# Two small bias loads and the first projection weights, moved to the tail of SyncE's start-up queue in a token-mixing transformer kernel

## The chip, the cores and the metric

The kernel runs on one core of one Trainium2 chip. The metric is device time in microseconds (us) for one execution of the whole kernel; lower is better. Before the change it is 1309.34 us, the median of 3 runs (1308.7 to 1309.64).

## What is computed

Input `x` has S = 2048 tokens of D = 1024 values in bfloat16. Four blocks follow one another, attention and token MLP in turn, with the same weights in both rounds:

```
x = x + A(layernorm(x), wqkv, wo)
x = x + B(layernorm(x), w1, b1, w2, b2)
x = x + A(layernorm(x), wqkv, wo)
x = x + B(layernorm(x), w1, b1, w2, b2)

A: qkv = x @ wqkv; 32 heads of 32 values; each token attends to itself and
   7 earlier tokens, 2 apart (positions s, s-2, ..., s-14); softmax; then @ wo
B: h = layernorm(x); u = gelu(h transposed @ w1 + b1)   (mixes over tokens, F = 3584)
   y = u @ w2 + b2; transposed back
```

`b1` has 3584 values and `b2` has 2048, both bfloat16. They are used in B alone: `b1` in the gelu, `b2` in the last sum. The first block that needs them is the second of the four.

## The kernel before

The tokens are cut into 16 tiles of 128 (even tokens first, then odd ones, because attention steps by two). A round has these stages: the projection to v for all 16 tiles; attention in 16 units, in which the q and k projections (`qk_chunk`, L345) of the next unit are interleaved with the scores and values of the present one; the output projection (`out_proj`, L435); the first MLP matrix (`gemm1`, L462) and the second (`gemm2`, L506). TensorE does all the products; ScalarE (ACT) and VectorE (DVE) empty its PSUM buffers and do softmax, gelu and layernorm; SyncE (SP) issues nearly all DMAs.

The change is in the first round's start (`start_up`, L202 to L319). It carries each token tile k through these steps, whose short names are functions in the code:

- `x_load` (L208): SP loads tile k of x, 256 KB (tile 0 in two halves). `w_load` (L217): SP loads a quarter of the v weights, 512 KB, tile name `wv`.
- `S_` (L221, twice per tile) and `A_` (L226): DVE computes mean and variance (`bn`, `mv`).
- `R_` (L230, through L172 and L173): ACT computes one over the standard deviation (`rs`).
- `N_` (L234, through L186): DVE normalises the tile in place.
- For tiles 0 to 4, `tr` (L239) transposes on TensorE (PE), and `C_` (L245) copies the result to `hT` on ACT. For tiles 5 to 15, `T_` (L263) is a transposing DMA, issued by SP, straight into `hT`.
- `V_` (L251): PE, 8 products for each half n of v. `E_` (L259): ACT empties that PSUM buffer (two buffers, tile name `m`).

Before any of this PE runs 14 warm-up products on zeros (L268).

The order on each engine is written out by hand: lists `pe`, `act`, `dve` and `sp` (L285 to L304) are worked off by the loop at L310, and `chain_` (L198) ties every step to the step issued before it on the same engine. So an engine can't do a later step of its list while it waits for an earlier one. Two things matter in the lists: DVE has `S_` of tile k + 1 (first half) ahead of `N_` of tile k, and ACT has a long run of `E_` and `R_` in turn.

What isn't tied by `chain_` is placed by the Tile framework's scheduler, where it finds the engine free by its own estimate. Before the change that holds for two things called right after `start_up` (L532 to L534):

- `load_qk(0)` (L337): SP loads the q and the k weights of the first four attention units, 512 KB each, tile name `wqk`. `qk_chunk` reads them when attention begins.
- `load_biases` (L138): GpSimd (POOL) issues the loads of `b1` and `b2` into bfloat16 tiles (`b_bf` in the profile), and DVE casts them to float32 (`b_sb`; L142 and L143). Both tiles lay a vector out over 128 partitions, 28 values of b1 and 16 of b2 in each, from a source in which neighbours in a partition lie 256 bytes apart (pairs of b2 excepted):

```
nc.gpsimd.dma_start(out=b1_bf[:], in_=B_b1.rearrange("(t p) -> p t", p=P))
nc.gpsimd.dma_start(out=b2_bf[:], in_=B_b2.rearrange("(i m c) -> m i c", m=P, c=DIL))
nc.vector.tensor_copy(out=b1_sb[:], in_=b1_bf[:])
nc.vector.tensor_copy(out=b2_sb[:], in_=b2_bf[:])
```

Later `load_qk` calls (L554) load the next weights as attention goes on; they aren't tied either. Weights of all kinds share a pool of 9 buffers. The last item on DVE's list is `zero_fill` (L149), which clears borders of attention's buffers.

Of the kernel before, what the change touches and what calls it, by code (L numbers as in the profile page):

```python
# [14 lines left out]
P = 128  # L15
# [3 lines left out]
DIL = 2  # L19
# [6 lines left out]
def kernel(  # L26
# [15 lines left out]
    nc = tc.nc  # L42
    x_in = A_x[0]
    out2d = out[0]
    S, D = x_in.shape
    F = B_w1.shape[1]
    KD = D // P
    FT = F // P
    NT = S // P
# [55 lines left out]
    def wt_(name, shape):  # L105
        return wp.tile(shape, BF16, name=name, tag="w")
# [4 lines left out]
    def ln_exp_table():  # L111
        return tc.keep_in_program_order(nc.scalar.preload_act_table_set("natural_log_exp_and_others"))
# [20 lines left out]
    b1_bf = const.tile([P, FT], BF16, name="b1_bf")  # L133
    b2_bf = const.tile([P, NI, DIL], BF16, name="b2_bf")
    b1_sb = const.tile([P, FT], FP32, name="b1_sb")
    b2_sb = const.tile([P, NI, DIL], FP32, name="b2_sb")

    def load_biases():  # L138
        with nc.allow_non_contiguous_dma(reason="tiny bias loads"):
            nc.gpsimd.dma_start(out=b1_bf[:], in_=B_b1.rearrange("(t p) -> p t", p=P))  # L140
            nc.gpsimd.dma_start(out=b2_bf[:], in_=B_b2.rearrange("(i m c) -> m i c", m=P, c=DIL))
        nc.vector.tensor_copy(out=b1_sb[:], in_=b1_bf[:])  # L142
        nc.vector.tensor_copy(out=b2_sb[:], in_=b2_bf[:])  # L143

    hT = pers.tile([P, KD, S], BF16, name="hT")
    qT = [pers.tile([P, S + PAD], BF16, name=f"qT{n}") for n in range(2)]
# [15 lines left out]
    wq_v = A_wqkv.rearrange("(kt p) c -> p kt c", p=P)  # L162
# [4 lines left out]
    def rows(t, c, i):  # L167
        return t[(c * NI + i) * P:(c * NI + i + 1) * P, :]
# [29 lines left out]
    def chain_(eng, f, *args):  # L198
        with tc.issue_after(last[eng].ins) if eng in last else nullcontext():
            last[eng] = f(*args)  # L200

    def start_up(v, wv):  # L202
        np_ = 5
        warm = x2("warm", [P, 512])
        nc.vector.memset(warm[:], 0.0)
        xs, tps, pss_, mvs, sts, rss = {}, {}, {}, {}, {}, {}
# [88 lines left out]
        dve = [(S_, 0, 0), (S_, 0, 1), (A_, 0)]  # L295
        for k in range(NT):
# [4 lines left out]
            if nx:  # L301
                dve += [(S_, k + 1, 1), (A_, k + 1)]
        dve.append((zero_fill,))
        sp = [(T_, k) for k in range(np_, NT)]  # L304
        qs = {"PE": pe, "ACT": act, "DVE": dve, "SP": sp}
        need = {R_: lambda k: k in mvs, N_: lambda k, h: k in rss, tr: lambda k: (N_, k) in done, C_: lambda k: k in tps,
                V_: lambda k, n, kts: ((C_, k) in done or (T_, k) in done), E_: lambda k, n: (V_, k, n) in done,
                T_: lambda k: (N_, k) in done}
        done = set()
        while any(qs.values()):  # L310
            for eng, q in qs.items():
                while q and (q[0][0] not in need or need[q[0][0]](*q[0][1:])):
                    f, *args = q.pop(0)
                    chain_(eng, f, *args)
                    if f is V_:
                        if args[2][-1] == KD - 1:
                            done.add((f, args[0], args[1]))
                    elif args:
                        done.add((f, args[0]))  # L319

    def load_wv():
        return [[wt_("wv", [P, KD // 2, 512]) for _ in range(2)] for _ in range(NDC)]

    def fill_wv(wv, n):
        for hf in range(2):
            nc.sync.dma_start(out=wv[n][hf][:],
                              in_=wq_v[:, hf * (KD // 2):(hf + 1) * (KD // 2), 2 * D + n * 512:2 * D + (n + 1) * 512])

    def v_proj(v, c, i, wv, ns):
        for n in ns:  # L330
            ps = m_tile()
            for kt in range(KD):
                nc.tensor.matmul(ps[:], lhsT=hT[:, kt, cols(c, i)], rhs=wv[n][kt // 4][:, kt % 4, :],  # L333
                                 start=(kt == 0), stop=(kt == KD - 1))
            nc.scalar.copy(out=v[c][i][:, n * 512:(n + 1) * 512], in_=ps[:])

    def load_qk(g2):  # L337
        ts = []
        for part in range(2):
            t = wt_("wqk", [P, KD, 256])  # L340
            nc.sync.dma_start(out=t[:], in_=wq_v[:, :, part * D + g2 * 256:part * D + (g2 + 1) * 256])
            ts.append(t)
        return ts

    def qk_chunk(u, wts, part, n):  # L345
        g, c = divmod(u, DIL)
# [14 lines left out]
    def in_order(f, *args):  # L361
        with tc.issue_after(last_pe[0].ins) if last_pe[0] is not None else nullcontext():
            last_pe[0] = f(*args)
# [61 lines left out]
    def load_wo():  # L425
        tiles = []
        for n in range(NDC):
            tiles.append([])
            for hf in range(2):
                t = wt_("wo", [P, NG // 2, 512])  # L430
                nc.sync.dma_start(out=t[:], in_=wo_v[:, hf * (NG // 2):(hf + 1) * (NG // 2), n * 512:(n + 1) * 512])
                tiles[n].append(t)
        return tiles

    def out_proj(c, i, oT, wo, res, dst, h2):  # L435
        xr = x2("xr")
        nc.sync.dma_start(out=xr[:], in_=res(c, i))
        xn = x2("xn")
        for n in range(NDC):
            ps = m_tile()  # L440
            xs_ = slice(n * 512, (n + 1) * 512)
            for g in range(NG):
                mm = nc.tensor.matmul(ps[:], lhsT=oT[g][:, cols(c, i)], rhs=wo[n][g // 4][:, g % 4, :],  # L443
                                      start=(g == 0), stop=(g == NG - 1))
            nc.vector.tensor_tensor(out=xn[:, xs_], in0=ps[:], in1=xr[:, xs_], op=ALU.add)  # L445
        nc.sync.dma_start(out=rows(dst, c, i), in_=xn[:])
        h2[c][i] = vhp.tile([P, D], BF16, name="h2", tag="vh")
        mean, rs = stats(xn, 1.0 + EPS, eps2)
        norm_act(h2[c][i][:], xn[:], mean, rs)
        return mm  # L450
# [47 lines left out]
    def load_w2(i):  # L498
        tiles = []
        for n in range(NW2):  # L500
            t = wt_("w2", [P, HF, 256])
            nc.sync.dma_start(out=t[:], in_=w2_v[:, n * HF:(n + 1) * HF, i * 256:(i + 1) * 256])
            tiles.append(t)
        return tiles
# [20 lines left out]
    for li in range(2):  # L525
        first = li == 0
        v = [[None] * NI for _ in range(DIL)]
        for c, i in order:
            v[c][i] = vhp.tile([P, D], BF16, name="v", tag="vh")
        wv = load_wv()  # L530
        if first:
            start_up(v, wv)  # L532
            wts = load_qk(0)
            load_biases()  # L534
            res = lambda c, i: xin_v[c, i]
        else:
            fill_wv(wv, 0)
            fill_wv(wv, 1)
            wts = load_qk(0)
            for i in range(NI):  # L540
                for c in range(DIL):
                    v_proj(v, c, i, wv, (0, 1))
            res = lambda c, i: rows(xb, c, i)
        oT = [gop.tile([P, S], BF16, name="oT", tag="go") for _ in range(NG)]
        h2 = [[None] * NI for _ in range(DIL)]
        chunks = [(0, 0), (0, 1), (1, 0), (1, 1)]
        last_pe[0] = None
        for part, n in chunks:
            in_order(qk_chunk, 0, wts, part, n)
        wo = None  # L550
        for vis in range(2 * NU):
            u, b = divmod(vis, 2)
            if b == 0 and u + 1 < NU and (u + 1) % (2 * DIL) == 0:
                wts = load_qk((u + 1) // (2 * DIL))  # L554
            if vis == 2 * NU - 6:
                wo = load_wo()
            in_order(scores, u, b)
            for n in range(2):
                if n and vis:
                    in_order(values, *divmod(vis - 1, 2), v, oT)  # L560
                if u + 1 < NU:
                    in_order(qk_chunk, u + 1, wts, *chunks[2 * b + n])
                else:
                    in_order(out_proj, 0, 2 * b + n, oT, wo, res, xa[li], h2)
        in_order(values, NU - 1, 1, v, oT)
        for c, i in order[4:]:
            out_proj(c, i, oT, wo, res, xa[li], h2)
        g = [None] * NFB
        for fb in range(NFB):
            gemm1(fb, h2, g)  # L570
        if first:
            ln_exp_table()
        for i in range(NI):
            w2t = load_w2(i)
            for c in range(DIL):
                gemm2(c, i, w2t, g, xa[li], rows(xb, c, i) if first else out_v[c, i], first)
# [30 lines left out]
```

The softmax here doesn't subtract the row's maximum and nothing guards it: scores larger than these inputs give would overflow.

## Time and profile before

| What | Value |
|---|---|
| Median of 3 runs | 1309.34 us |
| The profiled execution, its time | 1308.38 us |
| Its span, first to last instruction | 1306.7 us |
| PE busy | 1294.7 us (99%) |
| DVE busy, ACT busy, POOL busy | 392.6, 385.1, 4.3 us |
| DMA, mean rate | 93 GB/s |
| First step of attention's q, k products (L350) | 73.59 us after the span's start |

The profile is of one execution. Its engines are PE (products), PEld (weight loads of PE), DVE, ACT, POOL and SP. A row of the timeline gives the start in us from the span's start, the duration, the engine, the line, the operation, the tile written and those read, the shape and the count; in square brackets stands how long the engine had been idle before it and what ended that wait. "SPq" or "POOL" with DMA_DIRECT2D is the issue of a DMA, not its transfer; a DMA's landing is when its completion is seen. PE's busy time counts pipelined products whose ends are modelled, so a busy PE isn't always a PE at its full rate.

### The profile page before, as it was taken

How to read it: one execution, taken by the hardware profiler on the slowest of the kernel's cores; microseconds unless marked ns; L12 is line 12 of the kernel's file. 1: busy time of each engine (PE TensorE's matmuls, PEld its weight loads, DVE VectorE, ACT ScalarE, POOL GpSimd, SP SyncE). 2: the span in 40 equal slices, each digit the busy share in tenths (PEclk: the TensorE clock that was granted, in tenths of full speed). 3: DMA queues.
4: the chain of work that ended last, by engine and by line, in shares of the span. 5: the costliest groups of instructions: out<-in, count | busy, mean ns of one | idle time of the engine just before them, and what ended most of it. 6: DMA issues, size and time to landing. Idle time of an engine off the chain costs nothing.

```text
span 1306.7 us, 21044 instructions
## 1 busy us (share of the span) xinstructions
PE 1294.7 (99%) x9398; PEld 583.0 (45%) x9398; DVE 392.6 (30%) x654; ACT 385.1 (29%) x628; POOL 4.3 (0%) x13
## 2 busy tenths in 40 slices
PE   7999999999999999999999999999999999999998
PEld 3444444444444444444444444444444444444443
DVE  5436667930000013223210566688000000111111
ACT  4446776531111110000023677664211111000000
POOL 1000000000000000000000000000000000000000
PEclk8999999999999999999999999999999999999999
DMA  9521112452322227456431100144522222334320
GB/s 250 113 66 34 34 34 83 145 170 65 93 68 71 76 67 180 113 136 172 121 89 37 53 27 19 35 130 151 147 65 81 81 59 72 110 105 133 117 91 33
DMA packets 191290, 121.69 MB, mean 93 GB/s; under 512 B 33376, under 2 KB 172896, under 8 KB 191200
## 3 DMA queue, kind: packets, MB, share of 16 engines
q1 hardware_dynamic: 191088, 120.35, 32.6%
q8 instruction: 73, 1.20, 0.4%
q0 software_dynamic: 112, 0.01, 0.1%
q14 instruction: 17, 0.14, 0.0%
HBM read 96.48 MB, written 16.78 MB: 87 GB/s over the span
## 4 chain that ended last, share of the span: by engine, by line
PE 95%; DVE 2%; ACT 1%; DMA 1%; issue 0%; POOL 0%; POOLq 0%
PE m L350 18%; PE s L513 15%; PE s L470 15%; PE m L513 7%; PE m L470 7%; PE acc L470 7%; PE acc L513 7%; PE m L443 7%; PE m L333 4%; PE m L255 3%; PE acc L404 1%; PE s L376 1%; PE acc L408 1%; DMA b_bf<-in_B_b_dram 1%; DVE xn L445 1%; DVE x L186 0%
## 5 line engine op out<-in xcount | busy, mean ns | idle before, releaser
L513 PEld LDWEIGHTS <-w 128*128 128x128 bf16 x1792 | 175.4, 98 | 211.4
L470 PEld LDWEIGHTS <-w 128*128 128x128 bf16 x1792 | 175.3, 98 | 211.5
L350 PE MATMUL m<-hT,wqk 128*128 128x512 bf16 x1024 | 241.8, 380 | 0.0
L470 PE MATMUL s<-h,w 128*128 128x512 bf16 x896 | 202.8, 379 | 0.0
L513 PE MATMUL s<-g,w 128*128 128x512 bf16 x896 | 199.9, 379 | 0.0
L516 DVE SCALAR_TENSOR_TENSOR xo<-s,b_sb,xs 128x512 bf16<-128x512 f32 x32 | 24.0, 751 | 540.7 <-PE s L513 534.4
L350 PEld LDWEIGHTS <-wqk 128*128 128x128 bf16 x1024 | 90.5, 98 | 108.7 <-issue 12.9
L385 DVE TENSOR_TENSOR Pm<-pc,band 64x1152 bf16<-64x1152 bf16 x128 | 96.3, 752 | 65.1 <-ACT pc L380 63.1
L443 PE MATMUL m<-wo,oT 128*128 128x512 bf16 x512 | 112.2, 379 | 0.1
L380 ACT ACTIVATE pc<-s,shift 128x576 bf16<-128x576 f32 x128 | 87.8, 737 | 59.9 <-PE s L376 59.9
L470 PE MATMUL acc<-h,w 128*128 128x512 bf16 x448 | 103.9, 379 | 0.0
L513 PE MATMUL acc<-g,w 128*128 128x512 bf16 x448 | 100.6, 379 | 0.0
L513 PE MATMUL m<-g,w 128*128 128x512 bf16 x448 | 99.3, 379 | 0.0
L470 PE MATMUL m<-h,w 128*128 128x512 bf16 x448 | 99.0, 379 | 0.0
L172 ACT ACTIVATE ln<-mv,eps 128x1 f32<-128x1 f32 x64 | 18.9, 295 | 240.4 <-DVE mv L180 222.2
L477 ACT ACTIVATE g<-s,b_sb 128x1024 bf16<-128x1024 f32 x28 | 31.2, 1114 | 166.9 <-PE s L470 166.9
L443 PEld LDWEIGHTS <-oT 128*128 128x128 bf16 x512 | 49.4, 98 | 59.6 <-issue 1.3
L255 PE MATMUL m<-wv,hT 128*128 128x512 bf16 x256 | 58.0, 383 | 1.2 <-ACT hT L248 0.7
L422 DVE TENSOR_TENSOR oT<-acc,rd 128x512 bf16<-128x512 f32 x64 | 44.0, 687 | 39.6 <-ACT rd L420 39.6
L333 PE MATMUL m<-wv,hT 128*128 128x512 bf16 x256 | 55.4, 379 | 0.0
L356 DVE CAST qT<-m 128x512 bf16<-128x512 f32 x32 | 21.8, 682 | 83.1 <-PE m L350 83.1
L445 DVE TENSOR_TENSOR xn<-m,xr 128x512 bf16<-128x512 f32 x64 | 44.0, 688 | 8.0 <-PE m L443 6.6
(61 smaller groups left out, 631.7 us busy)
## 6 DMA issues: line engine op xcount, KB each, us to landing
w<-in_B_w_dram SPq DMA_DIRECT2D x56, 512.0 KB, 3.8
w<-in_B_w_dram SPq DMA_DIRECT2D x64, 448.0 KB, 4.5
wqk<-in_A_wqkv_dram SPq DMA_DIRECT2D x16, 512.0 KB, 5.6
xa<-xn SPq DMA_DIRECT2D x32, 256.0 KB, 2.0
xs<-xa SPq DMA_DIRECT2D x32, 256.0 KB, 3.2
wv<-in_A_wqkv_dram SPq DMA_DIRECT2D x8, 512.0 KB, 5.3
wo<-in_A_wo_dram SPq DMA_DIRECT2D x8, 512.0 KB, 4.8
xr<-in_A_x_dram SPq DMA_DIRECT2D x16, 256.0 KB, 3.0
```

The source lines that it names most:

```text
L255: r = nc.tensor.matmul(pss_[k, n][:], lhsT=hT[:, kt, cols(*order[k])], rhs=wv[n][kt // 4][:, kt % 4, :], start=(kt == 0), stop=(kt == KD - 1))
L333: nc.tensor.matmul(ps[:], lhsT=hT[:, kt, cols(c, i)], rhs=wv[n][kt // 4][:, kt % 4, :], start=(kt == 0), stop=(kt == KD - 1))
L350: mm = nc.tensor.matmul(ps[:], lhsT=wts[part][:, kt, (g % 2) * P:(g % 2 + 1) * P], rhs=hT[:, kt, lo:lo + 512], start=(kt == 0), stop=(kt = ...
L380: nc.scalar.activation(out=pc[:, 2 * n:2 * n + 2].rearrange("p h t k -> p h (t k)"), in_=ss[n][:, :, 0:HB * HW], func=ACT.Exp, scale=scale ...
L385: nc.vector.tensor_tensor(out=pm[rp, :, b * HB:(b + 1) * HB, r * HK:r * HK + HW], in0=pc[rp], in1=mk, op=ALU.mult)
L422: nc.vector.tensor_tensor(out=oT[g][:, lo:lo + hb * P], in0=acc[:, 0, :], in1=rd[:], op=ALU.mult)
L443: mm = nc.tensor.matmul(ps[:], lhsT=oT[g][:, cols(c, i)], rhs=wo[n][g // 4][:, g % 4, :], start=(g == 0), stop=(g == NG - 1))
L445: nc.vector.tensor_tensor(out=xn[:, xs_], in0=ps[:], in1=xr[:, xs_], op=ALU.add)
L470: nc.tensor.matmul(pairs[fl][0][dc], lhsT=wt[c][:, i, fl * P:(fl + 1) * P], rhs=h2[c][i][:, dc * 512:(dc + 1) * 512], start=(k == 0), stop ...
L477: nc.scalar.activation(out=g[fb][:, fl, :].rearrange("p (n d) -> p n d", n=2), in_=t[:], func=ACT.Gelu_apprx_tanh, bias=b1_sb[:, ft:ft + 1])
L513: nc.tensor.matmul(aps[dc], lhsT=w2t[ft // HF][:, ft % HF, c::DIL], rhs=g[ft // GF][:, ft % GF, dc * 512:(dc + 1) * 512], start=(ft == 0), ...
L516: nc.vector.scalar_tensor_tensor(out=xo[:, dc * 512:(dc + 1) * 512], in0=aps[dc], scalar=b2_sb[:, i, c:c + 1], in1=xs[:, dc * 512:(dc + 1) ...
```

## The change

The two bias loads go from POOL's queue to SP's, and out of the scheduler's hands: they become the last item of SP's hand-written list, behind the transposing DMAs of all tiles. The two casts become a step of their own, the last of DVE's list, behind `zero_fill`; the loop's table of conditions holds it back until the loads have been issued in program order. `load_qk(0)` is tied to SP's chain as well, behind the bias loads. `load_qk` fills a list that it is given and returns its last DMA, as `chain_` wants it; its two later calls do what they did. The loop's `done` set now also takes steps without arguments.

```diff
     def load_biases():
         with nc.allow_non_contiguous_dma(reason="tiny bias loads"):
-            nc.gpsimd.dma_start(out=b1_bf[:], in_=B_b1.rearrange("(t p) -> p t", p=P))
-            nc.gpsimd.dma_start(out=b2_bf[:], in_=B_b2.rearrange("(i m c) -> m i c", m=P, c=DIL))
+            nc.sync.dma_start(out=b1_bf[:], in_=B_b1.rearrange("(t p) -> p t", p=P))
+            return nc.sync.dma_start(out=b2_bf[:], in_=B_b2.rearrange("(i m c) -> m i c", m=P, c=DIL))
+
+    def cast_biases():
         nc.vector.tensor_copy(out=b1_sb[:], in_=b1_bf[:])
-        nc.vector.tensor_copy(out=b2_sb[:], in_=b2_bf[:])
+        return nc.vector.tensor_copy(out=b2_sb[:], in_=b2_bf[:])
...
         dve.append((zero_fill,))
-        sp = [(T_, k) for k in range(np_, NT)]
+        dve.append((cast_biases,))
+        sp = [(T_, k) for k in range(np_, NT)] + [(load_biases,)]
...
-        need = {R_: lambda k: k in mvs, ...
+        need = {cast_biases: lambda: (load_biases,) in done, R_: lambda k: k in mvs, ...
...
-                    elif args:
-                        done.add((f, args[0]))
+                    else:
+                        done.add((f, *args[:1]))
...
-    def load_qk(g2):
-        ts = []
+    def load_qk(g2, ts):
         for part in range(2):
-            t = wt_("wqk", [P, KD, 256])
-            nc.sync.dma_start(out=t[:], in_=wq_v[:, :, part * D + g2 * 256:part * D + (g2 + 1) * 256])
-            ts.append(t)
-        return ts
+            ts[part] = wt_("wqk", [P, KD, 256])
+            r = nc.sync.dma_start(out=ts[part][:], in_=wq_v[:, :, part * D + g2 * 256:part * D + (g2 + 1) * 256])
+        return r
...
             start_up(v, wv)
-            wts = load_qk(0)
-            load_biases()
+            wts = [None, None]
+            chain_("SP", load_qk, 0, wts)
```

More of the change, by code (lines that the diff above doesn't have):

```diff
@@ L303, in start_up @@
         dve.append((zero_fill,))
-        sp = [(T_, k) for k in range(np_, NT)]
+        dve.append((cast_biases,))
+        sp = [(T_, k) for k in range(np_, NT)] + [(load_biases,)]
         qs = {"PE": pe, "ACT": act, "DVE": dve, "SP": sp}
-        need = {R_: lambda k: k in mvs, N_: lambda k, h: k in rss, tr: lambda k: (N_, k) in done, C_: lambda k: k in tps,
+        need = {cast_biases: lambda: (load_biases,) in done, R_: lambda k: k in mvs, N_: lambda k, h: k in rss, tr: lambda k: (N_, k) in done, C_: lambda k: k in tps,
                 V_: lambda k, n, kts: ((C_, k) in done or (T_, k) in done), E_: lambda k, n: (V_, k, n) in done,
@@ L538 @@
             fill_wv(wv, 1)
-            wts = load_qk(0)
+            wts = [None, None]
+            load_qk(0, wts)
             for i in range(NI):
@@ L553 @@
             if b == 0 and u + 1 < NU and (u + 1) % (2 * DIL) == 0:
-                wts = load_qk((u + 1) // (2 * DIL))
+                wts = [None, None]
+                load_qk((u + 1) // (2 * DIL), wts)
             if vis == 2 * NU - 6:
```

## The prediction, on record before the result

> **What bounds the kernel now.** I read the page first, then the chain of waits for the first 80 us, then DVE's timeline at the start, then a table of windows, then SP's queue. The page says that PE is the engine to ask about:
>
> ```profile
> PE 1294.7 (99%) x9398; PEld 583.0 (45%) x9398; DVE 392.6 (30%) x654; ACT 385.1 (29%) x628; POOL 4.3 (0%) x13
> ```
>
> The change touches only the start, so what counts is whether the start is late. The chain of waits (start, duration, what) begins with a bias load, which is odd for data first read at 287.2 us (the gelu of L477):
>
> ```profile
> 1.37 8.74 DMA b_bf<-in_B_b_dram
> 10.46 0.30 ACT ln L172
> 11.03 0.43 DVE x L186
> 11.50 1.05 PE s L242 x8
> ...
> 45.97 27.79 PE m L255 x128
> ```
>
> DVE's timeline shows how. Statistics of tile 0 are done at 4.33; their aggregation (L228), which alone lets ACT and then the normalisation go on, starts at 10.22, because the cast of b1 stands ahead of it and waits 5.81 us for its load:
>
> ```profile
> 3.04 1.29 DVE L224 BATCH_NORM_STATS2 bn<-x 128x6 f32<-128x512 bf16 x2 [1.71 <-DMA x<-in_A_x_dram]
> 10.13 0.18 DVE L142 CAST b_sb<-b_bf 128x28 f32<-128x28 bf16 x1 [5.81 <-DMA b_bf<-in_B_b_dram]
> 10.22 0.20 DVE L228 BATCH_NORM_AGGREGATE mv<-bn 128x2 f32<-128x12 f32 x1
> ```
>
> The windows (stretch, length, busy time of PE, PEld, DVE, ACT, POOL, then granted clock, DMA share, GB/s) show the price: warm-up to 6.65, then 4.85 us in which PE does nothing while DMA crawls at 167 GB/s, then the v projection to 73.75:
>
> ```profile
> 1.40:6.65 5.25, 5.25 (x14) 1.77 (x14) 1.29 (x2) 0.69 (x1) 3.72 (x7) 1.00 0.92 210
> 6.65:11.50 4.85, 0.00 (x1) 0.01 (x1) 1.32 (x5) 0.50 (x2) 0.00 (x0) 0.74 1.16 167
> 11.50:18.58 7.08, 5.97 (x36) 3.29 (x37) 4.63 (x11) 3.41 (x9) 0.00 (x0) 0.69 1.07 370
> 18.58:73.75 55.17, 54.69 (x264) 24.77 (x262) 27.50 (x57) 25.41 (x62) 0.00 (x0) 1.00 0.60 138
> ```
>
> From 27 to 46 us the chain alternates between DVE (L186, L224, L228) and ACT with a period of 1.99 us per tile (22.31, ..., 41.49, 43.49); from 45.97 PE runs 128 products back to back. Both parts hang on tile 0's aggregation, so a shift there goes through to attention, and from there PE is full to the end.
>
> [...] So b1 is 3584 descriptors of 2 bytes and b2 1024 of 4 (pairs lie together); over 16 engines 224 + 64 = 288 each. [...] the software queue has 80 data packets, of 128 and 64 bytes for b1 and 256 for b2. [...] bias packets run from 5.64 to 10.04 us, and the second quarter of `wv` landed 4.33 us after the first (7.18, 11.51), though 512 KB take 1.36 us at the rate of the later x tiles (256 KB every 0.68 us). So the biases cost the stream 4.33 - 1.36 = 2.97 us, 10.3 ns per descriptor. [...] products are 0.43 us apart until 5.6, again from 13.2 to 15.1, and 0.216 from 16.0 on.
>
> **The change part by part.**
>
> *The cast leaves the head of DVE's queue.* Recomputing the start with the trace's own durations: aggregation of tile 0 at 4.41 instead of 10.22; ACT's two steps end at 5.2. DVE's list has the first statistics of tile 1 ahead of the normalisation, and tile 1 lands at 5.17: statistics 5.2 (was 10.34), normalisation 5.89 (was 11.03). The first transpose could start 0.47 later, at 6.36, but PE ends its warm-up at 6.65: it starts there, 4.85 us earlier than at 11.50. The idle window is gone.
>
> *The bias transfers leave the early stream.* Everything from the second `wv` quarter on comes about 3.0 to 3.3 us earlier: that quarter at about 8.3, x tile 2 (was 12.18) at about 9.0, the last `wv` quarter (was 15.87) near 12.5. These landings move less than 4.85, so one may become the new wait. First copy of tile 0: 7.3 to 8.4; first v products at 7.95, with `wv` there since 7.18 at the latest. Normalisation of tile 1 needs ACT's rs at 8.84, but in DVE's list it stands behind tile 2's first statistics: 9.0 + 0.66 = 9.68, against 14.10. **Next late is x tile 2**, and the gain is 4.42 here. Then PE's clock gives some back: its first transposes follow the warm-up directly, and if it is still at full clock at 10.3, tile 1's transposes take 0.62 instead of 1.05 and the gain is 4.42 + 0.43, about 4.85; if the clock has dropped, 4.4 or a little more. Tile 2's normalisation (was 17.52) follows tile 1's copy, so it carries that gain. Tile 4 is wanted at 13.7 and lands near 13.1. From there the 1.99 us rhythm and the 128 products are the same. I take 4.8.
>
> *The load of wqk moves* from 19.27 and 19.96 to behind the last transposing DMA. That one was issued at 46.69 and took 1.29: SP is free at 47.98 - 4.8 = 43.2. Nothing was queued behind the old place (SP was idle until 26.14), so leaving it saves nothing. It is wanted by L350, at 73.59 - 4.8 = 68.8. It takes 5.6 us from issue to landing (median of 16). So the biases ahead of it may take 68.8 - 43.2 - 5.6 = 20.0 us, which is 69 ns for each of 288 descriptors. Their price in SP's queue isn't in the trace. Below: 10.3 ns, as now, 3.0 us. Nearest row: two `wqk` loads issued together land 1.66 us apart, 64 descriptors of 512 bytes per engine, 26 ns each: 7.5 us. Above: [...] doubling 26 gives an estimate of 52 ns, 15.0 us. I take 7.5; at all three the cost is nothing, as it lies under the v products. A gain below nothing is excluded, since these loads are only added there.
>
> *SP's issue* of 3584 and 1024 descriptors: 1024 took 0.37 (wqk) to 1.29 us (transpose), so by scale 1.7 to 5.8 us for both, within the same cover. Behind them on SP stands only wqk until PE frees weight buffers (next issue at 71.20).
>
> *The casts* (0.18 + 0.16 us) wait on DVE behind the zero fill, until about 43 + 7.5 + 3 = 54. Behind them is the first q copy (L356, at 77.25, before which DVE idles 26.64 us). No cost; without that cover a late bias would hold that copy.
>
> *POOL* loses 1.68 + 0.92 us of issues ahead of the identity and band masks (3.18 to 5.44). PE wants the identity at 6.65; no gain.
>
> **Sum**, on the profiled execution: 1308.38 - 4.8 = 1303.6 (span 1301.9). That execution is 0.96 under the median of the runs, so median 1309.34 - 4.8 = **1304.5**.
>
> **Rivals.**
>
> *Transfers come no earlier.* If the dip in the stream isn't the biases' doing, x tile 2 still lands at 12.18, tile 1 is normalised at 12.86 instead of 14.10, and the gain is about 1.3: 1308.0. [...] Against: it ran at over 300 GB/s between 4.5 and 6 us, and the dip's limits are those of the bias packets.
>
> *The biases hold wqk too long* (ends slower). SP sends single elements at a price above 69 ns; L350 then waits at the start of attention. From 86 ns on ((20.0 + 4.8) / 288) the gain is gone. At 100 ns the biases take 28.8 us, wqk is 8.8 late, and the sum is +4.0: 1313.3. For it: the price isn't in the trace[...]. Against: it needs nearly three times the price of a 512-byte packet.
>
> *The change doesn't do what it says*: the scheduler puts another load, one that waits for PE to free a buffer, ahead of wqk on SP, or another wait takes the cast's place on DVE. The first is excluded by the chain only for the tied steps. It would cost about what it gains: 1309.
>
> **How the numbers follow.** About 0.2%, 2.6 us, is what a measurement can tell from no change here. Main forecast 0.82 (faster); transfers no earlier 0.06 (same); not what it says 0.04 (same); biases too long 0.08 (slower, a small part same, neglected). Ends: if x tile 2 comes at 8.3 the rs of tile 1 decides and 14.10 becomes 8.84, gain 5.3, with the clock's 0.43 some 5.7: 1303.6, less 0.4 for the scatter of runs (1308.7 to 1309.64): 1303.2. If PE drops to half clock for one window of 3.4 us on the way, half of that is lost: gain 3.1, 1306.2, plus 0.4: 1306.6. The range is 1303.2 to 1306.6.
>
> **What would show it.** Right: in the after profile tile 0's aggregation follows its statistics with no gap; the first transpose is at about 6.65; no dip between 6 and 10 us; `wv`'s second quarter lands near 8.3; tile 1 is normalised at 9.7 behind tile 2's landing; L350 starts at 68.8; bias loads follow the last transpose near 43. Wrong: a wait of L350 for wqk at the start of attention, any DVE wait for b_bf that something else queues behind, or a first normalisation still late.

## The result

| | Before | After |
|---|---|---|
| Median | 1309.15 us (4 runs, 1308.7 to 1309.64) | 1303.55 us (4 runs, 1303.29 to 1303.78) |
| Profiled execution, span | 1308.38, 1306.7 | 1303.29, 1301.6 |
| Attention's first products | 73.59 (L350) | 68.70 (L351) |

The ratio is 0.9957 (95% interval 0.994 to 0.9974). The median moved by 5.6 us, the profiled execution by 5.1, the start of attention in it by 4.89; the forecast was 4.8. In the changed file most lines are one to three numbers further down: L172, L186, L224, L228, L341 and L350 are now L174, L188, L226, L230, L343 and L351.

DVE's timeline of the changed kernel at the start:

```profile
3.00 1.29 DVE L226 BATCH_NORM_STATS2 bn<-x 128x6 f32<-128x512 bf16 x2 [1.67 <-DMA x<-in_A_x_dram]
4.32 0.21 DVE L230 BATCH_NORM_AGGREGATE mv<-bn 128x2 f32<-128x12 f32 x1
5.11 0.69 DVE L226 BATCH_NORM_STATS2 bn<-x 128x6 f32<-128x512 bf16 x1 [0.58 <-DMA x<-in_A_x_dram]
...
9.24 0.69 DVE L226 BATCH_NORM_STATS2 bn<-x 128x6 f32<-128x512 bf16 x1 [1.96 <-DMA x<-in_A_x_dram]
9.85 0.53 DVE L188 TENSOR_SCALAR x<-x,mv,rs 128x1024 bf16<-128x1024 bf16 x1
```

The aggregation follows its statistics with no cast between. But DVE waits again, at 9.24, for x tile 2: the new wait that was forecast. It holds tile 1's normalisation (9.85) although its rs has been there since 8.43. The chain of waits agrees; its first long piece is no longer a bias load, but the load of x tile 2, issued at 3.21 (start, duration, what):

```profile
3.21 6.00 DMA x<-in_A_x_dram
9.28 0.57 issue
9.85 0.54 DVE x L188
...
67.41 1.46 PE m L257 x6
68.87 6.91 PE m L351 x32
```

The windows (columns as in the prediction) show what became of the dead stretch:

```profile
1.40:6.65 5.25, 5.25 (x21) 2.11 (x22) 3.04 (x7) 1.18 (x3) 0.99 (x5) 1.00 0.80 258
6.65:11.50 4.85, 2.34 (x19) 1.13 (x18) 2.82 (x7) 1.87 (x5) 0.00 (x0) 1.00 1.02 322
11.50:18.58 7.08, 6.58 (x42) 3.22 (x42) 5.32 (x11) 4.46 (x13) 0.00 (x0) 1.00 1.06 383
```

From 6.65 to 11.50 the DMA engines move 322 GB/s where it was 167, PE works for 2.34 us where it did nothing, and its clock stays at 1.00 (it was 0.74, then 0.69). A profile's record of the clock begins with the first rise (at 5.61 before, at 5.00 here), so the 1.00 of the first row says nothing of the time ahead of it, in which products come 0.43 us apart, as against 0.216 later.

SP's queue at the tail, with the biases between the last transpose and wqk:

```profile
41.16 1.23 SPq L266 DMA_TRANSPOSE hT<-x  x1
42.45 0.57 SPq L140 DMA_DIRECT2D b_bf<-in_B_b_dram  x1
43.07 1.97 SPq L141 DMA_DIRECT2D b_bf<-in_B_b_dram  x1
45.09 7.74 SPq L343 DMA_DIRECT2D wqk<-in_A_wqkv_dram  x5
```

The biases land at 47.58 and 47.79, the two halves of wqk at 49.58 and 51.40, 17 us or more before attention wants them.

### The profile page after: what moved, and what is told of

Same layout as the page of the kernel before. It is cut to its first block, busy times and chain, and to the rows that moved or that the text cites. A ratio compares the mean times of both kernels' runs of the same rounds, so it can differ in the third digit from the quotient of the medians.

```text
span 1301.6 us, 20885 instructions
## 1 busy us (share of the span) xinstructions
PE 1279.8 (98%) x9240; PEld 581.9 (45%) x9398; DVE 392.8 (30%) x654; ACT 385.1 (30%) x628; POOL 1.7 (0%) x11
## 4 chain that ended last, share of the span: by engine, by line
PE 94%; DVE 3%; issue 1%; ACT 1%; DMA 0%; SPq 0%; another core or an unknown queue 0%
PE m L351 17%; PE s L514 15%; PE s L471 15%; PE acc L471 7%; PE m L471 7%; PE m L514 7%; PE acc L514 7%; PE m L444 7%; PE m L336 4%; PE m L257 2%; PE acc L405 1%; PE s L377 1%; PE acc L409 1%; DVE xn L446 1%; DVE x L188 0%
## 5 line engine op out<-in xcount | busy, mean ns | idle before, releaser
L351 PE MATMUL m<-hT,wqk 128*128 128x512 bf16 x963 | 231.0, 380 | 7.9 <-issue 7.0
L351 PEld LDWEIGHTS <-wqk 128*128 128x128 bf16 x1024 | 90.5, 98 | 108.7 <-issue 12.9
L174 ACT ACTIVATE ln<-mv,eps 128x1 f32<-128x1 f32 x64 | 18.9, 296 | 234.5 <-DVE mv L182 222.2
```

Of the source, the lines that this page charges most:

```text
L351: mm = nc.tensor.matmul(ps[:], lhsT=wts[part][:, kt, (g % 2) * P:(g % 2 + 1) * P], rhs=hT[:, kt, lo:lo + 512], start=(kt == 0), stop=(kt = ...
```

## The experiments

The theory: the gain is made of three parts that follow one another at the start, namely DVE's wait for the bias, the bias packets in the stream of x and `wv`, and PE's clock, which dropped while PE waited (a mean of 0.74 in the 4.85 us without work). The main rival: the wait on DVE is all, and where the transfers run makes no difference.

**biases_early_on_pool.** The loads go back to POOL at the start; the casts stay at the end of DVE's list (without their condition, which no longer has an object).

```diff
-            nc.sync.dma_start(out=b1_bf[:], in_=B_b1.rearrange("(t p) -> p t", p=P))
-            return nc.sync.dma_start(out=b2_bf[:], in_=B_b2.rearrange("(i m c) -> m i c", m=P, c=DIL))
+            nc.gpsimd.dma_start(out=b1_bf[:], in_=B_b1.rearrange("(t p) -> p t", p=P))
+            return nc.gpsimd.dma_start(out=b2_bf[:], in_=B_b2.rearrange("(i m c) -> m i c", m=P, c=DIL))
...
+        load_biases()
         wm = m_tile()
...
-        sp = [(T_, k) for k in range(np_, NT)] + [(load_biases,)]
+        sp = [(T_, k) for k in range(np_, NT)]
```

> As the changed kernel, but the two bias loads go back to POOL at the start (before the hand-written lists); the casts stay at the end of DVE's list. So the wait is gone and the transfers are early again. Theory (two effects, the stream becomes the next wait): the bias packets slow the stream between about 6 and 10 us as before, x tile 2 lands near 12.2 instead of 9.22, tile 1 is normalised near 12.9 instead of 9.85, and the kernel is some 3.0 us slower than the changed one plus up to 0.5 for a PE clock that has dropped: 1306.6 to 1307.1. Rival (the DVE wait is all, the stream has slack): as the changed kernel, 1303.6.

Measured: 1308.33 us (12 runs, 1307.08 to 1309.44), ratio to the kernel before 0.999 (0.9981 to 0.9999). The rival is out: with the wait gone but the transfers early, 0.9 us of the gain is left (0.1 to 2.5 by the interval). The stream is as it was (x tile 2 lands at 12.33), and tile 1 is normalised at 12.97, as expected. But the time is 1.2 to 1.7 us above what I had expected of it. DVE's timeline of this kernel shows the wait for x tile 2:

```profile
7.28 0.21 DVE L230 BATCH_NORM_AGGREGATE mv<-bn 128x2 f32<-128x12 f32 x1
12.36 0.69 DVE L226 BATCH_NORM_STATS2 bn<-x 128x6 f32<-128x512 bf16 x1 [4.87 <-DMA x<-in_A_x_dram]
12.97 0.53 DVE L188 TENSOR_SCALAR x<-x,mv,rs 128x1024 bf16<-128x1024 bf16 x1
```

Its windows show what came on top:

```profile
6.65:12.31 5.66, 1.49 (x11) 0.53 (x8) 0.81 (x2) 1.47 (x4) 0.00 (x0) 1.00 1.17 202
12.31:19.14 6.83, 5.58 (x26) 3.11 (x27) 4.43 (x9) 2.30 (x6) 0.00 (x0) 0.50 1.07 371
```

PE is busy for 1.49 of 5.66 us, and then its clock is at half for 6.83 us, while it has work. In this execution L351 starts at 73.90, no earlier than before. The clock that each run was granted, as a mean over its whole span (1.000 is full speed), orders the other executions the same way: the two runs at 0.999 took 1307.08 and 1307.67 us, the three at 0.998 took 1307.66 to 1307.83, the seven at 0.997 took 1308.13 to 1309.44.

**early_on_pool_pe_kept_busy.** The same, with products on zeros in PE's idle stretch; they write a PSUM buffer that nobody reads.

```diff
+        fm = a_tile()
+        def F_(n):
+            for _ in range(n):
+                r = nc.tensor.matmul(fm[:, 0, :], lhsT=warm[:, 0:P], rhs=warm[:], start=True, stop=True)
+            return r
...
-        pe = [(tr, 0), (V_, 0, 0, lo4), (tr, 1), ...
+        pe = [(tr, 0), (V_, 0, 0, lo4), (F_, 18), (tr, 1), ...
```

> As biases_early_on_pool (loads early on POOL, casts late; 1308.33), with 18 products on zeros put on PE between tile 0's first v products and tile 1's transposes, where PE waits for x tile 2; their results are read by nothing. Theory (in biases_early_on_pool PE's idle stretch of 5 us drops its clock, from 12.31 to 19.14 us in its profile, and that costs what my first expectation lacked): the clock stays up, tile 1 is normalised at 13.0 as before, L351 starts near 72.0 instead of 73.9, total 1306.6. Rival (the late stream alone costs it all): 1308.3.

Measured: 1306.58 us (12 runs, 1306.26 to 1307.08), ratio 0.998 (0.9971 to 0.9989), L351 at 71.83. The late stream alone doesn't cost it all: 18 products that compute nothing save 1.75 us (the kernel before, measured beside each of the two, took 1309.23 and 1309.26). Its windows, over the same stretches, differ from the last ones in PE's busy time and then in the clock:

```profile
6.65:12.31 5.66, 4.98 (x29) 2.30 (x27) 0.22 (x2) 1.47 (x4) 0.00 (x0) 1.00 1.17 211
12.31:19.14 6.83, 6.33 (x41) 2.90 (x40) 5.00 (x11) 3.89 (x10) 0.00 (x0) 1.00 1.07 373
```

**before_pe_kept_busy** and **after_pe_kept_busy.** The two kernels themselves, with PE kept busy in the same way: 35 warm-up products in place of 14 in the kernel before, `(F_, 7)` in the changed one.

```diff
-        for _ in range(14):
+        for _ in range(35):
...
-        pe = [(tr, 0), (V_, 0, 0, lo4), (tr, 1), ...
+        pe = [(tr, 0), (V_, 0, 0, lo4), (F_, 7), (tr, 1), ...
```

> The kernel before, with 35 warm-up products in place of 14, so that PE is busy while DVE waits for the bias: the wait and the early transfers stay, only the clock can't drop. Theory (the clock's share of the whole effect is what PE's idle stretch cost: tile 0's transposes and first 4 products at half rate, some 1.4 us on the path, in this profile[...]): tile 0's aggregation still at 10.2, L350 near 72.3 instead of 73.59, median 1307.8, scatter smaller than 0.8. Rival (the clock has no part in it): 1309.2, scatter as before.

Measured: 1308.16 us (12 runs, 1307.53 to 1309.74), ratio 0.9993 (0.9985 to 1.0002). The difference of 1.07 us lies the way the theory has it, but its interval reaches 1, so its size is open; L350 starts at 73.11, where I had expected 72.3. The scatter is not smaller as I had expected: the bias load lands at 10.11 in the profile of before and at 10.56 here, and everything behind it moves along.

> As the changed kernel, with 7 products on zeros in the same place, where PE waits 1.84 us. Theory (in some executions the clock drops for one window there, as in after_again's profile from 11.19 to 14.60, in others it doesn't): L351 at 68.7 in every execution, median 1303.3, with the scatter of the runs under 0.6. Rival (the drop costs nothing or the products delay tile 1): 1303.6 or more, scatter as before.

Measured: 1303.47 us (4 runs, 1303.15 to 1303.76), L351 at 68.69. Against 1303.6 for the changed kernel this can't be told from no change.

**after_again.** The changed kernel once more, unedited.

> The changed kernel once more, on this chip, as the measure for the other three: 1303.5, within 0.4.

Measured: 1303.6 us (4 runs, 1303.16 to 1304.47), ratio 0.9957 (0.9942 to 0.9972). Its profile is the execution of 1304.47, and shows what makes one execution of this kernel slower than another:

```profile
6.65:11.19 4.54, 1.88 (x17) 0.93 (x15) 2.35 (x6) 1.47 (x4) 0.00 (x0) 1.00 1.00 325
11.19:14.60 3.41, 3.41 (x12) 1.36 (x10) 2.32 (x6) 2.05 (x5) 0.00 (x0) 0.50 1.07 382
```

PE was busy for 1.88 of 4.54 us, and the clock fell for 3.41 us; L351 starts at 69.90 instead of 68.70. In the first profile of the same kernel the clock never fell. The other three runs here, and the four of the result, were granted 1.000 and took 1303.16 to 1303.78; this one was granted 0.998.

**biases_early_on_sp.** The biases stay on SP, but stand right behind the first quarter of `wv`.

```diff
         chain_("SP", w_load, 0, 0)
+        chain_("SP", load_biases)
...
-        sp = [(T_, k) for k in range(np_, NT)] + [(load_biases,)]
+        sp = [(T_, k) for k in range(np_, NT)]
```

> As the changed kernel, but the bias loads stand in SP's list right behind the first quarter of wv; casts at the end of DVE's list. Theory (what costs is 288 short descriptors per DMA engine ahead of wv and x, on whichever queue; 10.8 ns each in the changed kernel's trace, 3.1 us): second wv quarter near 11.6, x tile 2 near 12.3, tile 1 normalised near 13.0, total 1306.6 to 1307.2. Rival (only POOL's software queue hurts the stream): x tile 2 at 9 to 10, total 1303.6 to 1304.2.

Measured: 1308.13 us (20 runs, 1307.04 to 1309.1), ratio 0.9991 (0.9984 to 0.9997). The second `wv` quarter lands at 11.34, x tile 2 at 12.01, tile 1 is normalised at 12.64: as on POOL. So it isn't POOL's queue alone that hurts the stream: the same descriptors ahead of it on SP do as much. How they do it on SP is not shown. The issue of the second bias load took SP 3.33 us (from 3.22), so the second `wv` quarter was issued at 6.59 instead of 2.67, while the bias packets ran on the DMA engines until about 8; either could set the landing. On POOL, where SP issued that quarter at 2.67, only the DMA engines are left: from 6 to 10 us of the kernel before they moved 101 GB/s, with 91 bias packets among 482. In time the run misses the expected band by 0.9 us, and its profile has the cause seen above: the clock is at half from 10.94 to 17.77. The six runs granted 0.999 took 1307.04 to 1307.56 us, the fourteen at 0.997 took 1307.65 to 1309.1.

**wqk_untied.** The first wqk loads aren't tied.

```diff
-            chain_("SP", load_qk, 0, wts)
+            load_qk(0, wts)
```

> As the changed kernel, but the first wqk loads aren't tied behind the biases; the scheduler puts five wqk loads among the transposing DMAs again. Theory (the move of wqk costs and gains nothing): 1303.3 to 1303.9, L351 starts at 68.7 as in the changed kernel, though transposes land later. Rival (the transposes' delay by wqk loads was part of what the start waited for): slower by 1 us or more, 1304.6 or above.

Measured: 1303.94 us (4 runs, 1303.41 to 1304.85), ratio 0.996 (0.9945 to 0.9975); after_again, measured beside it, has 1303.6. L351 starts at 69.83 in an execution whose clock fell (granted 0.998), against 69.90 in the profile of after_again, which had the same. Of the four runs the two granted 1.000 took 1303.41 and 1303.47, the two at 0.998 1304.41 and 1304.85. The move of wqk costs and gains nothing that can be measured.

**biases_x6** and **biases_x12.** The pair of loads stands at SP's tail 6 and 12 times; all but the last pair go into a spare buffer.

```diff
+            bx = x2("bx")
+            for k in range(5):
+                o = k * (FT + NI * DIL)
+                nc.sync.dma_start(out=bx[:, o:o + FT], in_=B_b1.rearrange("(t p) -> p t", p=P))
...
             nc.sync.dma_start(out=b1_bf[:], ...
```

> As the changed kernel, but SP loads both biases 6 times in all at the tail, five times into a spare buffer that nothing reads. The price from the changed kernel's trace is 3.1 us for one pair of loads. Theory (the cover is about 20 us): 6 x 3.1 = 18.7, wqk's first half lands near 49.6 + 15.6 = 65.2, before L351 wants it at 68.7: 1303.6, no change. Rival (the price grows when many are queued, or SP's own issue adds up): L351 late, above 1305.

Measured: 1304.33 us (3 runs, 1302.84 to 1304.83), ratio 0.9958 (0.9943 to 0.9973). The first half of wqk lands at 66.76, the second, which is read later, at 68.58, and L351 starts at 68.38 without a wait: six times the load is still covered, with little to spare. The profiled run, 1302.84, was granted a clock of 1.000, the two longer ones 0.998.

> The same with 12 pairs of bias loads, 11 into the spare buffer. Theory (beyond the cover each pair costs its whole 3.1 us): wqk's first half lands near 49.6 + 34.2 = 83.8, L351 starts there instead of at 68.7, so 15.1 us late: 1318.7, slower than the kernel before. Rival (the bias transfers share the DMA engines with wqk, which slips past them): 1303.6 to 1306.

Measured: 1324.23 us (2 runs, 1323.4 and 1325.05), ratio 1.0112 (1.0093 to 1.013). This is the slower rival of the prediction, made to happen. PE's timeline at the end of the v projection:

```profile
59.83 9.01 PE L262 MATMUL m<-wv,hT 128*128 128x512 bf16 x41
86.32 8.96 PE L356 MATMUL m<-hT,wqk 128*128 128x512 bf16 x30 [17.48 <-DMA wqk<-in_A_wqkv_dram]
```

And the windows of this kernel, before, during and after that wait:

```profile
42.00:68.70 26.70, 26.70 (x125) 11.93 (x123) 2.93 (x4) 8.79 (x15) 0.00 (x0) 1.00 0.84 14
68.70:86.30 17.60, 0.14 (x1) 0.00 (x0) 0.35 (x2) 0.59 (x1) 0.00 (x0) 0.65 0.83 53
86.30:91.05 4.75, 4.73 (x12) 1.70 (x13) 0.00 (x0) 0.59 (x1) 0.00 (x0) 0.50 1.16 291
```

While the biases run, the DMA engines are over 80% busy and move 14 GB/s. Two terms exceed what I had expected. wqk lands at 86.28, not 83.8: from 6 to 12 pairs its landing moves by 86.28 - 66.76 = 19.52, so a pair costs 3.25 us, not 3.1. SP issues the pairs without a break, some 3.2 us each, so whether its issue or the DMA engines set this price isn't told apart. And the wait drops the clock, so that 4.75 us of attention run at half rate, some 2.4 us lost. 17.6 + 2.4 = 20.0; the profiled execution is 1323.4 - 1303.29 = 20.1 above that of the changed kernel.

**x2_ahead_of_wv** and **x2_ahead_rs_later.** The changed kernel's next waits, removed. The first puts x tile 2 ahead of the second quarter of `wv` on SP, and tile 4 ahead of the third; the second also lets ACT empty a PSUM buffer before it waits for a tile's variance.

```diff
         chain_("SP", w_load, 0, 0)
-        chain_("SP", w_load, 0, 1)
         chain_("SP", x_load, 2)
+        chain_("SP", w_load, 0, 1)
         chain_("SP", x_load, 3)
+        chain_("SP", x_load, 4)
...
-            if j + 8 < NT:
-                act.append((R_, j + 8))
+            if j >= 2 and j + 6 < NT:
+                act.append((R_, j + 6))
```

> As the changed kernel, but SP loads x tile 2 ahead of the second wv quarter, and x tile 4 ahead of the third. Theory (in the changed kernel the start waits for x tile 2, landing at 9.22, while rs of tile 1 is there at 8.43): x tile 2 lands near 7.5, tile 1 is normalised near 8.5 instead of 9.85, L351 starts near 67.3 instead of 68.7, total 1302.2. Rival (another wait follows at once, the later wv quarters or PE's clock): within 0.4 of the changed kernel.

Measured: 1302.72 us (5 runs, 1302.35 to 1302.79), ratio 0.9946 (0.9932 to 0.996): 0.8 to 0.9 below the changed kernel, where I expected 1.3. x tile 2 lands at 7.75, so the wait on it is gone. In the profiled execution the clock rose only at 6.97, so the warm-up lasted longer, tile 0's transposes began at 7.16 and tile 1's normalisation at 9.34, not 8.5; L351 starts at 68.21.

> As the run before, and on ACT the steps R_ of tiles 8 to 15 stand two places later among the E_ steps, so that ACT empties a PSUM buffer before it waits for a tile's variance. Theory (between 22 and 41 us the v projection runs at 1.99 us per 8 products, because ACT waits 0.98 us for DVE in each turn; 26 groups take 46.3 us where 26 x 1.727 = 44.9): 1.4 us less than the run before, total 1300.8. Rival (PE isn't held by ACT there, the gaps of 0.39 us before weight loads are hidden): as the run before.

Measured: 1301.11 us (5 runs, 1300.39 to 1301.41), ratio 0.9934 (0.9922 to 0.9947), L351 at 66.20. It beats both kernels, by 8.2 us (1309.28 in the same runs) and some 2.5. ACT's timeline in the changed kernel:

```profile
28.08 0.29 ACT L174 ACTIVATE ln<-mv,eps 128x1 f32<-128x1 f32 x1 [0.99 <-DVE mv L230]
28.41 0.20 ACT L175 ACTIVATE rs<-ln 128x1 f32<-128x1 f32 x1
28.52 0.57 ACT L263 CAST v<-m 128x512 bf16<-128x512 f32 x1
30.07 0.29 ACT L174 ACTIVATE ln<-mv,eps 128x1 f32<-128x1 f32 x1 [0.99 <-DVE mv L230]
```

And in x2_ahead_rs_later:

```profile
26.56 0.59 ACT L263 CAST v<-m 128x512 bf16<-128x512 f32 x1 [1.14 <-PE m L257]
27.05 0.30 ACT L174 ACTIVATE ln<-mv,eps 128x1 f32<-128x1 f32 x1
27.38 0.20 ACT L175 ACTIVATE rs<-ln 128x1 f32<-128x1 f32 x1
28.29 0.59 ACT L263 CAST v<-m 128x512 bf16<-128x512 f32 x1 [0.71 <-PE m L257]
```

In the first the step that empties PE's buffer (L263) comes every 1.99 us and stands behind a wait for DVE; in the second it comes every 1.73 us and waits for PE alone.

## Why the prediction was right

The forecast was 1304.5 us with a range of 1303.2 to 1306.6, and 1303.55 was measured. In the two profiled executions, from which the sum was worked out, the start of attention moved by 4.89 us where 4.8 was forecast. That closeness is in part luck, as two misses offset each other: tile 1's normalisation moved by 4.25, not 4.42, and the clock gave 0.64 behind it, not 0.43. The medians moved by 5.6, which puts the time near the low end of the range; the prediction had reached that end by another way, with x tile 2 landing at 8.3.

*The cast at the head of DVE's queue, and what is late next.* Both held. Aggregation 4.32 (forecast 4.41), first transpose 6.18 (6.65; the clock rose at 5.00 instead of 5.61, so the warm-up was shorter, 4.96 us against 5.26), x tile 2 at 9.22 (9.0), tile 1's normalisation 9.85 (9.68), L351 68.70 (68.8). The place of the next wait was read from the order of two items in DVE's list and the landing of one load, less what the biases had cost it; list and landing were in the trace of before. Later loads came 0.7 to 0.8 after their forecast (the last `wv` quarter at 13.24, not 12.5; x tile 4 at 13.93, not 13.1), and nothing waited for them.

*The transfers.* This was the larger part. biases_early_on_pool has the landings of the rival "transfers come no earlier" (x tile 2 at 12.33, tile 1 normalised at 12.97; the rival said 12.18 and 12.86). That its time, 1308.33, is near the rival's 1308.0 is chance: the clock's drop, which the rival didn't have, is in it. With PE kept busy, so that the clock dropped in none of the three profiles, the steps can be told apart: 1308.16 with wait and early transfers, 1306.58 without the wait, 1303.47 with the transfers moved too, and the runs of the three don't overlap. So, taken away in this order, the wait is worth 1.6 us and the stream 3.1, which is close to what the dip was priced at in the prediction (2.97). From 1309.23 to 1303.47 it is 5.8: these two, and 1.1 from 1309.23 to 1308.16 for the clock, a size that its interval doesn't resolve.

*The clock* is the term that the prediction sized too small. I gave it 0.43, for one group of transposes. In the two profiles it comes to 0.64: from tile 1's normalisation to the copy behind its transposes took 1.89 us before (14.10 to 15.99) and 1.25 after (9.85 to 11.10), because at half clock the products ahead of the transposes ended late as well: the first four took 1.89 us before and 1.04 in the changed kernel. The 3.4 us of a drop, on which the upper end of the forecast's range rests, is what after_again then showed (3.41), but in the profile of before the clock was at half for 6.83 us. In other executions of the kernel before it costs more. Each of its 71 runs beside the experiments was granted a mean clock of 0.995 to 0.997: the 47 at 0.997, as the profiled one, have a median of 1309.05 us, the ten at 0.995 one of 1310.06, while the four of the changed kernel were granted 1.000. The profiled execution, 1308.38, lies at the low end even of the 47, so the shift read from it understates that of the medians. The clock isn't all of that scatter: with PE kept busy before_pe_kept_busy still spreads over 2.2 us, and the landing of the bias, which everything waits for there, may be the rest; that isn't shown. The same miss shows in both experiments with early biases, where I allowed up to 0.5; on POOL, keeping PE busy saved 1.75.

*The price of the biases on SP* was given as 10.3 to 52 ns per descriptor, with 26 taken. The changed kernel's packet records have each of b1's 3584 elements as a packet of its own, of 2 bytes, which those of before, with up to 128 bytes in a packet, could not show. The biases' packets run from 43.6 to 46.6: 3.05 us for 288 descriptors per engine, 10.6 ns (10.8 in the expectations, from 3.1), and 11.3 in the steady row of twelve. The low end was right; the high one, the author's estimate by doubling the 26 ns of a 512-byte packet, was too high by a factor of nearly five for these loads. Their issue took SP 2.5 us, inside the 1.7 to 5.8 allowed. At the price measured, 3.25 us for a pair, the slower rival was far away: the cover ends near (68.7 - 49.58) / 3.25 = 5.9 more pairs, and six in all still fit.

*The move of wqk* at no cost: confirmed by wqk_untied and by biases_x6.

## What to carry to other kernels

A tiny load can cost twice at a start: by a wait in an engine's queue ahead of the first useful step, and by its descriptors in the stream that this step needs; moving only the wait gained 0.9 of 5.6 us here, as the stream stayed late and PE's clock, behind the wait for it, was at 0.50 for 6.83 us. Count a strided load's descriptors, not its bytes: here 11 KB in elements and pairs held the stream up as long as 1.2 MB of x would have (3.1 us at 256 KB per 0.68 us). Then ask which load lands last for the next item in each queue: that was worth another 0.8 us here, and a wait that stood ahead of a buffer's release on ACT another 1.6.

## What the runs showed of the hardware

Loads of 2 and 4 bytes per descriptor cost about the same from SP's queue as from POOL's: 10.6 and 11.3 ns per descriptor and DMA engine from SP, and 10.3 from POOL, the last worked out from the late landing of a `wv` quarter and not from packets. From SP they are means over bursts: in the middle of b1's load in the changed kernel the 16 engines start 272 packets in 0.1 us (44.8 to 45.3), which is one in 5.9 ns on each, and the rest of the time goes to the slow beginnings of the two loads.

PE's granted clock fell in some profiles where PE had little work at the start, and held in others:

| Run | Stretch, us from the span's start | PE busy in it, us | Granted clock behind it |
|---|---|---|---|
| `before` | 6.65 to 9.02 | 0.00 of 2.37 | 0.50 for 6.83 us |
| biases_early_on_pool | 6.65 to 12.31 | 1.49 of 5.66 | 0.50 for 6.83 us |
| after_again | 6.65 to 11.19 | 1.88 of 4.54 | 0.50 for 3.41 us |
| `after` | 6.65 to 11.50 | 2.34 of 4.85 | 1.00 |
| x2_ahead_rs_later | 6.65 to 12.31 | 4.07 of 5.66 | 1.00 |
| early_on_pool_pe_kept_busy | 6.65 to 12.31 | 4.98 of 5.66 | 1.00 |

The clock was still at half when PE had work again: PE was busy for 3.41 of the 3.41 us in after_again, and for 5.58 of the 6.83 in biases_early_on_pool. In biases_x12 the wait at the start of attention left PE busy for 0.14 of 17.60 us; the mean clock in it was 0.65, and 0.50 in the 4.75 us of work behind it. How much work holds the clock up isn't shown: the stretches differ in length, and the busy time has modelled ends. The changed kernel, unedited, gave both outcomes, with 2.34 of 4.85 us in its first profile and 1.88 of 4.54 in after_again.

With idle stretches of 2 to 5 us at the start, runs of one kernel scattered by up to 2.4 us (biases_early_on_pool); with PE kept busy in the two kernels without the bias wait, by 0.8 and 0.6.
